# Opening of an attention-plus-SwiGLU kernel: two load queues, one kvz evacuation, num/den ahead, filler matmuls, and weights gated by k

## The chip, the cores and the metric

The kernel runs on one core of one Trainium2 chip. The metric is device microseconds of one execution. "Before" has a median of 342.39 us. A "span" is the time between the first and last instruction of the profiled execution; it is about 2 us shorter than the time of the same run.

## The reference, cut to what matters

```python
def phi(x, c, s):                       # c, s: cos and sin of pi/2 * position / 576
    r = np.maximum(x, 0.0)
    return np.concatenate([r * c, r * s], axis=-1)      # 64 -> 128 features
kv  = np.einsum('bhsf,bhsd->bhfd', phi(k), v)           # 8 batches, 8 heads, 576 positions
z   = np.sum(phi(k), axis=2)
num = np.einsum('bhsf,bhfd->bhsd', phi(q), kv)
den = np.einsum('bhsf,bhf->bhs', phi(q), z)[..., None] + 1e-06
x   = (num / den)                                       # -> 4608 tokens x 512
xn  = x / rms(x) * rms_g
out = (silu(xn @ w_gate) * (xn @ w_val)) @ w_out        # 512 -> 1536 -> 512
```

## The kernel before

The program is a short opening for batch 0 and then a long stretch in which TensorE (PE in the profile) works on the gate, value and output matmuls, with the attention of the later batches between them. In the opening nothing can overlap with an earlier batch. Its steps are: load q, k and v; scale q (`qp`), transpose it on PE (`tps`), copy it out (`qpT`); scale k (`kp`), cast v (`vv`); compute k times v with z as a 65th column (`kvz`), copy it out (`kvzs`); compute numerator and denominator of four 128-row tiles (`nd`), divide (`den`, `rec`, `xt`), take the sum of squares (`scr`, `rs`), normalise (`xn`), transpose (`tpx`), copy (`xnT`); then the first gate and value matmuls, 128 columns at a time.

```python
    for e in range(4):
        load_piece("q", q, 0, 2 * e, 2, nc.sync)          # all loads on SyncE's queue
    for e in range(2):
        load_piece("k", k, 0, HH * e, HH, nc.sync)
    # ... the 64 last rows of k and v, then four pieces of v, then rms_g ...
    nc.gpsimd.tensor_copy(out=gate[:, :], in_=raws["v", 0][:, 2, 0:1])   # weights wait for v
    load_wgv(0)                                            # 512 columns of w_gate and of w_val
    load_wgv(512)
    load_first("q", 1)
    load_first("k", 1)
    # ... tables; PSUM pools: gv 2 x 2 banks, acc 2 x 1, att 1 x 2 ...
    q_scale(0, 0, V, A); q_scale(0, 1, V, A); q_scale(0, 2, V, A)
    q_tr_pe(0, 0); q_out(0, 0, V)
    q_scale(0, 3, V, A)
    for j, eng in ((1, A), (2, V), (3, A)):
        q_tr_pe(0, j); q_out(0, j, eng)
    # ... k_prep and v_prep, shared by VectorE (V) and ScalarE (A) ...
    for e in range(4):                                     # two heads, evacuate, two heads, ...
        kvz(0, 2 * e, 2)
        kvz_out(0, e % 2, V if e % 2 else A, slice(e // 2, e // 2 + 1))
    nd(0, 0); x_of(0, 0)                                   # one PSUM buffer ("att") for nd
    nd(0, 1); x_of(0, 1)
    nd(0, 2); xn_scale(0, 0); x_of(0, 2)
    # ... xn_tr_pe, xn_out, nd(0, 3), x_of(0, 3), first_steps(0 to 3) interleaved ...
```

## Time and profile before

| what | value | where |
|---|---|---|
| time, median | 342.39 us | runs |
| PE busy over the span | 92% | page |
| PE busy from 0 to 25 us | 9.3 us of 25 | windows of 5 us |
| last piece of q lands | 6.63 us | landing times in the trace |
| kvz of batch 0, four rounds with evacuations | 14.87 to 19.22 us | chain of waits |
| first full-width (512-column) gate matmul | 31.46 us | chain of waits |

The windows view gives, for each stretch in us, the busy time and instruction count of each engine, then the granted PE clock (1.00 is full), the DMA share and GB/s. Its column heads and three rows of the kernel before:

```profile
core 0: us, PE busy (x) PEld busy (x) DVE busy (x) ACT busy (x) POOL busy (x), PEclk, DMA share, GB/s
15.00:20.00 5.00, 3.25 (x48) 2.64 (x45) 1.04 (x4) 0.97 (x3) 2.65 (x4) 0.50 1.18 191
20.00:25.00 5.00, 2.08 (x25) 1.49 (x26) 4.02 (x11) 1.63 (x5) 1.12 (x2) 0.50 1.25 209
25.00:30.00 5.00, 4.95 (x61) 4.62 (x59) 2.85 (x6) 3.20 (x8) 3.09 (x5) 0.64 1.05 396
```

PE is busy 3.25 and then 2.08 us of 5, at half clock, and still mostly at half clock when it has enough to do from 25 us on. Pieces of the chain of waits of the kernel before (start us, duration us, what):

```profile
15.56 0.28 ACT kvzs L149
...
15.88 0.72 PE kvz L226 x10
...
19.26 0.61 PE nd L255 x8
...
19.90 0.18 DVE den L265
...
20.10 0.21 DVE rec L270
...
20.34 0.70 DVE xt L273
...
21.09 0.64 PE nd L255 x8
...
26.65 0.42 PE vps L341 x4
...
31.46 0.38 PE gps L341
```

Each kvz round waits for the copy of the round before, and each nd waits for the division of the tile before, since both use the same PSUM buffer. Four 128-column matmuls take 0.42 to 0.43 us, 0.107 us each.

### The profile page before, as it was taken

Reading aid. Unit: us, or ns where it says so; the run is one execution under the profiler, and the core shown is the slowest. Engines: PE = TensorE matmul, PEld = TensorE weight load, DVE = VectorE, ACT = ScalarE, POOL = GpSimd, SP = SyncE. Lnnn points to the kernel's source line nnn. Section 1 sums busy time; section 2 is a strip of 40 time slices with the busy share of each in tenths; the row PEclk is TensorE's granted clock in tenths of the full one; section 3 lists DMA queues with packets and bytes.
Section 4 is the critical chain, followed back from the end, with each engine's and each line's share of the span. In section 5 each row is a group of like instructions: output and inputs, shape, how many; then the busy total and the mean of one; then the engine's idle time right before and its main releaser. Section 6 shows DMA issues by size and latency. Waiting matters only on the chain.

```text
span 340.3 us, 5633 instructions
## 1 busy us (share of the span) xinstructions
PE 313.8 (92%) x2060; PEld 159.3 (47%) x2096; DVE 193.1 (57%) x423; ACT 152.3 (45%) x300; POOL 40.8 (12%) x69
## 2 busy tenths in 40 slices
PE   1459999899899998999999999999999999999994
PEld 1447555455445444544544455445544444444441
DVE  4754577766687896589268945792674132132300
ACT  4626773864444463443444444444443223323221
POOL 0528451101100110110011001100110000000000
PEclk9858999999999999999999999999999999999999
DMA  7999998448849799659948895691113100000024
GB/s 236 242 215 310 297 341 247 120 109 280 297 112 215 185 188 231 201 129 233 243 130 162 187 259 173 138 205 64 45 32 64 62 31 33 31 31 34 31 63 92
DMA packets 81757, 53.59 MB, mean 157 GB/s; under 512 B 52097, under 2 KB 75137, under 8 KB 81729
## 3 DMA queue, kind: packets, MB, share of 16 engines
q1 hardware_dynamic: 74864, 40.91, 46.2%
q0 software_dynamic: 6864, 12.32, 14.4%
q8 instruction: 16, 0.26, 0.3%
q14 instruction: 13, 0.10, 0.1%
HBM read 38.01 MB, written 9.44 MB: 139 GB/s over the span
## 4 chain that ended last, share of the span: by engine, by line
PE 78%; DVE 12%; ACT 3%; issue 3%; DMA 1%; SPq 0%; DVEq 0%; ACTq 0%
PE gps L341 24%; PE vps L341 24%; PE acc L378 20%; PE kvz L226 3%; DVE hT L350 3%; DVE xt L273 3%; PE nd L255 3%; DVE xn L294 2%; DVE kp L142 2%; PE acc L649 2%; PE tps L197 1%; ACT scr L281 1%; ACT sil L349 1%; DMA raw<-in_q_dram 1%; DVE rec L270 1%
## 5 line engine op out<-in xcount | busy, mean ns | idle before, releaser
L350 DVE TENSOR_TENSOR hT<-vps,sil 128x512 bf16<-128x512 f32 x108 | 74.5, 691 | 106.8 <-PE vps L341 77.5
L341 PE MATMUL gps<-xnT,wg 128*128 128x512 bf16 (+1 forms) x437 | 111.3, 370 | 1.2 <-issue 0.2
L341 PE MATMUL vps<-xnT,wv 128*128 128x512 bf16 (+1 forms) x447 | 111.5, 370 | 0.5
L378 PE MATMUL acc<-wo,hT 128*128 128x512 bf16 x378 | 96.6, 379 | 1.7 <-DVE hT L350 1.5
L349 ACT ACTIVATE sil<-gps 128x512 bf16<-128x512 f32 x108 | 63.3, 591 | 66.1 <-PE gps L341 61.8
L341 PEld LDWEIGHTS <-wv 128*128 128x128 bf16 x456 | 44.1, 99 | 50.0
L341 PEld LDWEIGHTS <-wg 128*128 128x128 bf16 x456 | 41.7, 99 | 40.8 <-issue 0.2
L378 PEld LDWEIGHTS <-hT 128*128 128x128 bf16 x384 | 37.5, 98 | 47.2 <-DVE hT L350 2.5
L281 ACT ACTIVATE scr<-xt 128x513 bf16<-128x513 f32 x36 | 22.9, 635 | 65.0 <-DVE xt L273 65.0
L286 POOL TENSOR_TENSOR rs<-ssq,mhalf 128x1 f32<-128x1 f32 x36 | 20.1, 557 | 195.5 <-ACT scr L281 195.5
L149 ACT COPY osb<-acc 128x512 f32<-128x512 f32 x34 | 19.9, 584 | 25.6 <-PE acc L378 23.6
L294 DVE SCALAR_TENSOR_TENSOR xn<-xt,rs,gb 128x512 bf16<-128x512 f32 x36 | 26.7, 743 | 0.8 <-POOL rs L286 0.8
L273 DVE TENSOR_TENSOR xt<-nd,rec 128x512 f32<-128x512 f32 x36 | 24.9, 691 | 1.2
L255 PEld LDWEIGHTS <-qpT 128*128 128x128 bf16 x256 | 12.6, 102 | 11.5 <-DVE xt L273 3.6
L255 PE MATMUL nd<-kvzs,qpT 128*128 128x65 bf16 x256 | 14.2, 200 | 3.6 <-DVE xt L273 3.0
L142 DVE TENSOR_SCALAR qp<-raw,cos_tab 128x512 bf16<-128x512 f32 x32 | 15.0, 480 | 3.5 <-DMA raw<-in_q_dram 3.5
L226 PE MATMUL kvz<-vv,kp 128*128 128x65 bf16 x256 | 12.0, 199 | 4.5 <-DVE vv L151 3.4
L149 ACT CAST vv<-raw 128x512 bf16<-128x512 f32 x26 | 14.8, 619 | 2.6 <-DMA raw<-in_v_dram 2.6
L142 DVE TENSOR_SCALAR kp<-raw,cos_tab 128x512 bf16<-128x512 f32 x32 | 15.2, 482 | 0.0
L226 PEld LDWEIGHTS <-kp 128*128 128x128 bf16 x320 | 11.8, 101 | 6.7 <-ACT kp L140 3.5
L197 PE MATMUL tps<-ident,qp 128*128 128x128 bf16 x64 | 6.3, 265 | 7.7 <-ACT qp L140 7.5
L649 PE MATMUL acc<-wo,hT 128*128 128x512 bf16 x46 | 11.4, 379 | 0.1
(65 smaller groups left out, 154.7 us busy)
## 6 DMA issues: line engine op xcount, KB each, us to landing
out_dram<-osb SPq DMA_DIRECT2D x32, 256.0 KB, 2.5
raw<-in_q_dram SPq DMA_DIRECT2D x20, 256.0 KB, 4.0
raw<-in_v_dram SPq DMA_DIRECT2D x20, 256.0 KB, 3.3
raw<-in_k_dram SPq DMA_DIRECT2D x16, 256.0 KB, 4.5
raw<-in_k_dram SPq DMA_DIRECT2D x4, 512.0 KB, 6.2
raw<-in_q_dram POOLq DMA_DIRECT2D x2, 1024.0 KB, 12.3
raw<-in_k_dram POOLq DMA_DIRECT2D x2, 1024.0 KB, 13.7
raw<-in_v_dram POOLq DMA_DIRECT2D x2, 1024.0 KB, 10.7
```

Source lines behind the costliest of these rows:

```text
L142: nc.vector.tensor_scalar(out=dst, in0=src, scalar1=tab[lanes, col : col + 1], scalar2=0.0, op0=ALU.mult, op1=ALU.max,)
L149: nc.scalar.copy(out=dst, in_=src)
L226: nc.tensor.matmul(kvz_ps[b][:, h // 2 % 2, c0 : c0 + DE], lhsT=kp[:, c, h, :], rhs=vv[:, c, h, :] if c < NJ else vvr[:, b % 2, h, :], sta ...
L255: nc.tensor.matmul(ps[rows, h // HH, (h % HH) * DE : (h % HH + 1) * DE], lhsT=src[:, h, cols], rhs=kz[:, h, :], start=True, stop=True,)
L273: nc.vector.tensor_tensor(out=xt[:, 0:DM].rearrange("p (g h d) -> p g h d", g=2, d=D), in0=ndv[:, :, :, 0:D], in1=rec[:, :].rearrange("p ( ...
L281: nc.scalar.activation(out=scr[:, :], in_=xt[:, :], func=AF.Square, scale=DM**-0.5, accum_out=ssq[:, :],)
L286: nc.gpsimd.tensor_tensor(out=rs[:, :], in0=ssq[:, :], in1=mhalf[:, :], op=ALU.pow)
L294: nc.vector.scalar_tensor_tensor(out=t[:, :], in0=xt[:, 0:DM], scalar=rs[:, 0:1], in1=gb[:, :], op0=ALU.mult, op1=ALU.mult,)
L341: nc.tensor.matmul(ps[:, c0 : c0 + n], lhsT=w[:, dt, nn * P : (nn + 1) * P], rhs=xnTs[blk][:, dt, c0 : c0 + n], start=(dt == 0), stop=(dt ...
L349: nc.scalar.activation(out=sil[:, :], in_=gps[:, :], func=AF.Silu)
L350: nc.vector.tensor_tensor(out=hTs[blk][:, nn, :], in0=vps[:, :], in1=sil[:, :], op=ALU.mult)
L378: nc.tensor.matmul(acc[:, :], lhsT=hTs[blk][:, nn, j * P : (j + 1) * P], rhs=wo[:, nn, :], start=(nn == 0), stop=(nn == NNT - 1),)
```

## The change

Its intent is to shorten the opening. q and k of batch 0 go over two queues (SyncE's and ScalarE's). kvz of all heads runs in one go, with one evacuation; the kept layout of `kvzs` follows PSUM, so that the later batches too evacuate in one instruction instead of two. PSUM pools are opened and closed so that num/den of batch 0 has three buffers and can run ahead of the division. Filler matmuls on a tile of zeros keep PE busy. The weight loads wait for k, which is loaded before v, and come in smaller chunks first.

```diff
-        load_piece("q", q, 0, 2 * e, 2, nc.sync)
+        load_piece("q", q, 0, 2 * e, 2, nc.scalar if e % 2 else nc.sync)
-        load_piece("k", k, 0, HH * e, HH, nc.sync)
+        load_piece("k", k, 0, HH * e, HH, nc.scalar if e % 2 else nc.sync)
-    nc.gpsimd.tensor_copy(out=gate[:, :], in_=raws["v", 0][:, 2, 0:1])
-    load_wgv(0)
+    nc.gpsimd.tensor_copy(out=gate[:, :], in_=raws["k", 0][:, HH, 0:1])
+    load_wgv(0, 256)
+    load_wgv(256, 256)
+    def keep_warm(n, pool="fill"):
+        ps = pools[pool].tile([P, SM], FP32, name="fill", tag=pool)
+        for _ in range(n):
+            nc.tensor.matmul(ps[:, :], lhsT=ident[:, :], rhs=zeros[:, :], start=True, stop=True)
+    with open_psum("fill", 1) as pools["fill"]:
+        keep_warm(12)
         ... q_scale, q_tr_pe, q_out as before, with
+            keep_warm(2)                  # before each of the transposes 1, 2 and 3
+        keep_warm(8)                      # after them
         ... k_prep, v_prep as before ...
-    for e in range(4):
-        kvz(0, 2 * e, 2)
-        kvz_out(0, e % 2, V if e % 2 else A, slice(e // 2, e // 2 + 1))
-    nd(0, 0); x_of(0, 0); nd(0, 1); x_of(0, 1); nd(0, 2); ... nd(0, 3); ...
+    with open_psum("nd", 2) as pools["nd"]:
+        kvz(0, 0, H, "nd")
+        kvz_out(0, V)
+        keep_warm(2, "acc")
+        nd(0, 0, "nd"); nd(0, 1); nd(0, 2, "nd")
+        x_of(0, 0); x_of(0, 1)
+        nd(0, 3)
+        x_of(0, 2)
+        keep_warm(8, "acc")
+    pools["gv"] = ctx.enter_context(open_psum("gv", 2))
     ... xn, transposes and first_steps follow, each first_steps one transpose later ...
-                kvz_out(b, 0, A)          # later batches
-                kvz_out(b, 1, V)
+                kvz_out(b, A)
```

(The diff is cut: the change of the `kvzs` index in `nd` and the order of the last x and xn are left out.)

## The prediction

> What bounds the kernel now. The kernel is a short opening (batch 0 loaded, q transposed, kvz, num/den, normalisation) and then a long TensorE stretch. The stretches of 5 us show PE busy 4.9 to 5.0 of 5 us from 25 us on; from 0 to 25 us it is busy only about 9 of 25. The first full-width step starts at 31.46 us (timeline, chain of waits). After that the kernel is PE-bound (page: PE 92%), so what ends the opening earlier comes off the end nearly one for one, if the loads keep up.
>
> The opening in the chain of waits: q lands at 6.63 us; q scaling, transposes and their copies, then k and v preparation on VectorE and ScalarE until 14.8; kvz in four rounds, each 0.72 us of PE and 0.28 to 0.30 of evacuation, 14.87 to 19.26 (4.4 us); three rounds of num/den, each waiting for the one PSUM buffer (nd 0.62, den 0.18, rec 0.21, xt 0.70: 1.85 us) to 24.78; then PE work at half clock. The windows give a granted clock of 0.50 from 15 to about 28.6 us: 8 transposes take about 0.85 us there and 0.45 later.
>
> What the change does, costed:
> 1. Two load queues. Issues on SyncE are 0.46 us each, and the DMA rate sags to about 200 GB/s from 3.5 to 5.2 us against 380 later. I expect q 0.7 to 1.2 us earlier (5.5 to 5.9). ScalarE's table load (1.28 us) moves behind three issues, still in time.
> 2. Fillers. 12 from about 2.3 us, cold some 5 us, can hold the first transposes by up to 1 us, but bring full clock by 6 to 9 us. [...] the clock rises at 28.6 after a window with PE about 98% busy, and the windows before it, 45 to 65% busy, did not raise it. Transposes and copies: about 1 us less.
> 3. kvz in one go: 1.25 us (as for batch 1 at 50.68) plus one evacuation, estimate 0.75 us from 0.29 (130 columns) and 0.44 (260): 2 us in place of 4.4.
> 4. num/den ahead: VectorE becomes the bound: 4 x 1.13 (x) + 4 x 0.75 (xn) = 7.5 us plus the tail, all PE work hidden at full clock.
> 5. Weights gated by k instead of v: about 3 us earlier[...]. v can land no earlier than the 13.5 of now, perhaps later: I charge 0.5 us.
>
> Sum: kvz starts about 13.5 (14.87), ends evacuated 15.6 (19.2), last xn about 23.5 (28.8), full-width steps start at 26.2 (31.46). Batch 1's single evacuation on ScalarE saves another 0.2. The later loads (first chunk of w_gate to w_out) stay continuous and come some 3 us earlier; their slack now is 3.5 to 9 us, so I expect no new wait. Gain about 5.3 us: 337.1 us, range 335.0 to 339.6.
>
> What would show it: clock 1.0 from some point before 10 us and no 0.50 later; kvz evacuation near 0.75 us; VectorE without gaps from kvz to the last xn; the first full-width gate matmul at 25.5 to 27; the rest of the trace merely shifted.
>
> What would make it wrong: weights starving v (kvz starting after 15); clock lost again in the idle time before kvz; fillers delaying the transposes; q of batch 1 landing later than its use at about 27 us; ScalarE, not VectorE, pacing k.
>
> Chances: faster by over 2% 0.15, within 2% 0.83, slower 0.02.

The 0.5 us charged in term 5 is guess alone, with no number behind it. The "6 to 9 us" of term 2 is an estimate. It can be worked out from the kernel before, whose clock records lie 3.41 us or a multiple of it apart (11.56, 14.97 and 28.63): one or two such steps after the start of the fillers at 2.3 us.

## The result

The changed kernel took 337.74 us (337.35 to 338.36, 4 runs) against 342.39 us, a ratio of 0.9862 with a 95% interval of 0.9841 to 0.9884. Ratios here are the mean time of one kernel's fast runs over that of the other's of the same rounds, so not quite the ratio of the medians that are quoted. The prediction of 337.1 us, in a range of 335.0 to 339.6 and most likely within 2%, held.

The same rows of the windows view of the changed kernel:

```profile
15.00:20.00 5.00, 2.88 (x55) 1.96 (x52) 3.76 (x11) 1.45 (x4) 2.90 (x5) 1.00 1.40 197
20.00:25.00 5.00, 3.88 (x53) 3.08 (x51) 3.64 (x7) 3.00 (x7) 3.24 (x6) 1.00 1.21 252
25.00:30.00 5.00, 4.98 (x51) 3.25 (x49) 2.26 (x4) 3.06 (x6) 3.52 (x5) 1.00 1.06 370
```

The clock is full in these three stretches (its first record in this trace, at 6.22 us, is a rise), and VectorE is busy where it was idle (3.76 us in place of 1.04 from 15 to 20 us). The chain of waits of the changed kernel:

```profile
2.27 4.68 PE fill L463 x12
6.96 0.45 PE tps L198 x8
...
12.99 1.08 ACT vv L150 x2
...
14.13 1.38 PE kvz L230 x40
...
15.53 0.71 DVE kvzs L152
...
16.29 0.42 PE nd L258 x8
...
19.38 1.73 PE fill L463 x8
21.11 0.24 PE tpx L318 x4
...
27.04 1.02 PE gps L344 x4
```

The first full-width matmul starts at 27.04 us, 4.42 us earlier. From there on the trace is the old one, shifted: the twelve products of gate and value of batch 0 (`hT` on VectorE) are each 4.43 us earlier than in the old trace, nearly all of the next block 4.68, the last 4.76. The step from 4.43 to 4.68 is batch 1, whose two evacuations ran one after the other before (0.38 us on ScalarE, then 0.44 on VectorE, in the chain of waits at 51.95 us) and are one now.

So in this pair of executions 4.4 of the 4.8 us come from the opening. The open questions were which parts of the change earn them, and why the opening was 0.8 us longer than predicted (27.04 in place of 26.2). Two theories of the gain were tested. Theory 1: the clock earns most of it, and the restructuring little. Theory 2: the removed waits earn it, and the fillers are decoration.

### The profile page after: what moved, and what is told of

It reads as the page before. It is cut to its first block, busy times and chain, and to the rows that moved or that the text cites. A ratio compares the mean times of both kernels' runs of the same rounds, so it can differ in the third digit from the quotient of the medians.

```text
span 335.6 us, 5731 instructions
## 1 busy us (share of the span) xinstructions
PE 318.9 (95%) x2132; PEld 157.9 (47%) x2132; DVE 190.6 (57%) x416; ACT 153.0 (46%) x298; POOL 43.1 (13%) x71
## 3 DMA queue, kind: packets, MB, share of 16 engines
q10 hardware_dynamic: 1072, 1.05, 0.9%
## 4 chain that ended last, share of the span: by engine, by line
PE 80%; DVE 12%; ACT 4%; issue 2%; DVEq 0%; ACTq 0%
PE gps L344 24%; PE vps L344 24%; PE acc L381 21%; DVE hT L353 3%; PE kvz L230 3%; DVE xt L276 3%; PE fill L463 2%; DVE xn L297 2%; PE nd L258 2%; PE acc L664 2%; ACT sil L352 1%; ACT scr L284 1%; PE tps L198 1%; DVE rec L273 1%; DVE kp L143 1%
## 5 line engine op out<-in xcount | busy, mean ns | idle before, releaser
L258 PEld LDWEIGHTS <-qpT 128*128 128x128 bf16 x256 | 11.5, 97 | 9.8 <-issue 2.4
L258 PE MATMUL nd<-kvzs,qpT 128*128 128x65 bf16 x256 | 12.9, 193 | 2.2 <-DVE xt L276 1.8
L463 PE MATMUL fill<-zeros,ident 128*128 128x512 bf16 x36 | 10.8, 444 | 2.3 <-DVE warm L411 2.3
L230 PE MATMUL kvz<-vv,kp 128*128 128x65 bf16 x256 | 10.8, 193 | 2.3 <-ACT vv L150 2.3
L230 PEld LDWEIGHTS <-kp 128*128 128x128 bf16 x320 | 10.7, 97 | 4.4 <-ACT vv L150 2.8
```

What stands on the lines that cost most here:

```text
L230: nc.tensor.matmul(kvz_ps[b][:, slot_of(h)[0], c0 : c0 + DE], lhsT=kp[:, c, h, :], rhs=vv[:, c, h, :] if c < NJ else vvr[:, b % 2, h, :], ...
L258: nc.tensor.matmul(ps[rows, h // HH, (h % HH) * DE : (h % HH + 1) * DE], lhsT=src[:, h, cols], rhs=kz[:, slot_of(h)[0], slot_of(h)[1], :], ...
```

## The experiments

In every experiment the number read from the profiled execution is the start of the first full-width gate matmul, called F below (31.46 us before, 27.04 in the changed kernel). The part of the span behind F is nearly the same in all traces (308.5 to 309.1 us), so nearly all of the spread between the runs of a kernel, 1 us and more, lies in the opening and is in F: one F stands for its execution, not for its kernel. The profiled execution of the kernel before took 342.11 us, faster than six of the seven that were run beside experiments 1 to 4 (341.84 to 343.51). Where one execution's F and the times of several runs disagree, both are told.

### 1. The changed kernel without fillers

```diff
     def keep_warm(n, pool="fill"):
-        ps = pools[pool].tile(...); for _ in range(n): nc.tensor.matmul(...)
+        return
```

> The changed kernel with every filler matmul taken out, all else kept. Theory 1 (the clock carries most of the gain): the granted clock is 0.5 for most of the opening, kvz takes about 2.3 us in place of 1.38, the 128-column gate and value matmuls run at about 107 ns, and the first full-width step starts at 29.5 to 30.5 us in place of 27.04: 340.2 to 341.3 us. Theory 2 (the removed waits carry it, the fillers are decoration, since VectorE paces num/den and x): at most 1 us later, 338 to 338.8 us.

Measured: 340.59 us (339.90 to 341.82), 0.994 of before (0.9907 to 0.9973); F = 30.88 us. The chain of waits of this run:

```profile
14.62 2.37 PE kvz L230 x40
...
22.32 0.62 PE tpx L318 x4
...
24.19 0.43 PE vps L344 x4
...
30.88 1.02 PE gps L344 x4
```

kvz takes 2.37 us in place of 1.38, and the small gate and value matmuls 0.107 us each. VectorE delivers the first xn at 22.27 us, but PE then needs 8.5 us (22.32 to 30.86) for what takes it 5.9 us in the changed kernel. Without the clock, the waits that the change removes win 0.6 us of the 4.4 in this pair of executions, and about 2.1 us (0.9 to 3.2) by the times of all runs (the ratio 0.994 and its interval, applied to 342.9 us). Theory 2 falls: it expected 338.8 us at most. (Not all of F's loss is the clock: VectorE's seven k instructions took 3.45 us here and 3.17 in the changed kernel.) (The windows view prints a clock of 1.00 for 10 to 25 us of this run, though its first clock record is at 29.2 us: a stretch before the first record is printed as full. The durations of the matmuls show the truth.)

### 2. The kernel before with fillers alone, twice

```diff
+    keep_warm(12)                          # into the still unused "att" buffer
     ...
     for j, eng in ((1, A), (2, V), (3, A)):
+        keep_warm(2)
         q_tr_pe(0, j); q_out(0, j, eng)
+    keep_warm(8)                           # second try: keep_warm(18)
     ...
+    keep_warm(2, "acc")                    # before nd(0, 0) and after nd(0, 0), (0, 1), (0, 2)
```

> The kernel before with fillers alone (12 first, 2 before each later transpose, 8 after, 2 around each num/den), all waits, the single queue and the order kept. Theory 1: the clock stays at 1.0 from 6 or 7 us on, the first full-width step comes 3 to 3.8 us earlier, at 27.7 to 28.5 us: about 338.6 to 339.4 us. Theory 2: PE still waits in each of the four kvz rounds and for the one num/den buffer, so at most 1 us is won: 341.4 us or more.

Measured: 340.86 us (340.47 to 341.60), 0.9947 (0.9922 to 0.9972); F = 30.96. By the trace's clock records (each has the time of a change and the new clock) it rose at 8.0 us, fell at 14.85, just as kvz began, and rose again only at 21.7: the fillers ended at 12.8 us, and PE was then idle until 14.85. The test of theory 1 was spoiled, so it was repeated with 18 fillers there.

> The kernel before with fillers again, now 18 in place of 8 after the q transposes, so that PE isn't idle before kvz (in the first try the clock fell at 14.85 us after an idle window). Theory 1 (clock): 1.0 from before 10 us on without a break, kvz rounds 0.40 us in place of 0.72, the first full-width step at 27.8 to 28.8 us (31.45 before): 338.7 to 339.8 us. Theory 2 (waits): it stays above 30 us even at full clock: 341 us or more.

Measured: 340.43 us (340.16 to 340.83), 0.9928 (0.9911 to 0.9945); F = 29.58, with full clock from 4.9 us on. The chain of waits:

```profile
15.00 0.47 PE kvz L227 x10
...
15.49 0.28 ACT kvzs L150
...
15.81 0.47 PE kvz L227 x10
...
29.58 0.38 PE gps L342
```

The clock alone wins 1.9 us by F, less than theory 1 expected (2.7 to 3.7), and about 2.5 us (1.9 to 3.1) by the times. So neither theory holds by itself: neither half earns what both earn together, 4.4 us by F, and by the times 4.7 us (4.0 to 5.4) in the first call of the changed kernel and 4.1 (3.4 to 4.7) in a second one (experiment 5). Whether the two are worth more together than the sum of each is not shown. The single executions say so (0.6 and 1.9 against 4.4), the times do not (2.1 and 2.5 against 4.1 to 4.7); the execution of the kernel before that F is compared with was a fast one, and the one without fillers (341.17 us) the second slowest of its four. What the traces do show is why neither half suffices: with the old order PE waits for evacuations that the clock didn't shorten (0.28 us on ScalarE at half clock in the kernel before, 0.28 at full clock in this run); with the new order and the old clock PE has its inputs earlier and becomes the bound itself.

### 3. The last eight fillers

In the changed kernel's chain the first xn transpose starts at 21.11 us, when the last eight fillers end, though its xn was ready at 20.59 (the timeline has it from 19.85 for 0.74 us). Do they only cost?

```diff
-        keep_warm(8, "acc")
```

> The changed kernel without the last 8 fillers, which in its trace hold the first xn transpose until 21.11 us though xn was ready at 20.6. If they only cost: clock still 1.0, the transpose starts at 20.65 and the first full-width step 0.3 to 0.5 us earlier (26.6): about 337.3 us. Rival (they keep the clock): the clock falls to 0.5 after 19 us and the first full-width step comes 1 us or more later: 338.7 us or more.

Measured: 341.25 us (339.40 to 342.71), 0.9953 (0.9911 to 0.9995); F = 31.94. But this execution had another trouble first. The VectorE timelines of the changed kernel and of this run, over the preparation of k:

```profile
9.81 1.80 DVE L143 TENSOR_SCALAR kp<-raw,cos_tab 128x512 bf16<-128x512 f32 x4
11.53 0.61 DVE L143 TENSOR_SCALAR kp<-raw,sin_tab 128x512 bf16<-128x512 f32 x1
```

```profile
10.72 3.01 DVE L143 TENSOR_SCALAR kp<-raw,cos_tab 128x512 bf16<-128x512 f32 x4
13.65 0.82 DVE L143 TENSOR_SCALAR kp<-raw,sin_tab 128x512 bf16<-128x512 f32 x1
```

Four instructions took 3.01 us in place of 1.80. In the same stretch GpSimd issued the weight loads, and the GpSimd timeline has an issue of w_val at 0.76 us here, at 0.92 us in the changed kernel:

```profile
10.49 0.76 POOL L127 DMA_DIRECT2D wv<-in_moe_w_val_dram  x1
```

One engine's instructions are longer where the other's are shorter. What causes this was not shown. In the changed kernel the same engines overlap in the same stretch, and VectorE isn't slowed that much (0.47 to 0.61 us an instruction). k was then late, kvz started only at 17.13 us, and the clock had been lost at 14.9, after a window of 3.41 us with PE busy 1.17 us of it (34%). The question about the fillers was put again with the weights gated by v, which takes GpSimd's work out of that stretch.

### 4. Weights gated by v again

```diff
-    nc.gpsimd.tensor_copy(out=gate[:, :], in_=raws["k", 0][:, HH, 0:1])
-    load_wgv(0, 256)
-    load_wgv(256, 256)
+    nc.gpsimd.tensor_copy(out=gate[:, :], in_=raws["v", 0][:, 2, 0:1])
+    load_wgv(0)
```

> The changed kernel with the weights gated by the second v piece and loaded in chunks of 512 columns again, as before. Theory: the first weights land by about 20.5 us, before their first use at 22.0, and the later loads have slack, so the first full-width step stays at 27.0 and the time within 0.3 us of the changed kernel: 337.5 to 338.1 us. Rival (the opening ends earlier only because the weights do): the first gate matmuls wait for a load, 1 to 3 us later, 338.7 to 340.7 us.

Measured: 337.25 us (336.74 to 338.59), 0.9843 (0.9805 to 0.988); F = 27.37. The first weights landed at 17.9 and 21.4 us, before their first use at 22.34, and no gate matmul waited for a load. So gating by k buys nothing in this opening. In this execution the seven k instructions took 2.98 us, as in the kernel before.

> Weights gated by v again (as the changed kernel was run before, at 337.25 us), and the last 8 fillers out. If those fillers only cost: clock stays 1.0 from before 10 us on, the first xn transpose starts about 0.4 us earlier relative to the last num/den, and the first full-width step at 26.9 to 27.1 us (27.37 with them): about 336.9 us. Rival (they keep the clock): it falls back to 0.5 near 20 to 23 us and the time is 338.5 us or more.

Measured: 338.86 us (338.75 to 340.02), 0.9888 (0.9867 to 0.9909); F = 28.23. The first xn transpose did start earlier, at 21.02 (21.45 with the fillers), but the clock was halved from 21.18. Windows of this run, cut at its clock records and in steps of 3.41 us from them (experiment 5 tells where this length is from):

```profile
14.36:17.77 3.41, 2.71 (x66) 2.21 (x66) 1.61 (x5) 0.25 (x1) 3.15 (x4) 1.00 1.06 165
17.77:21.18 3.41, 0.58 (x11) 0.47 (x12) 3.24 (x10) 2.17 (x6) 1.12 (x2) 1.00 1.24 207
21.18:24.60 3.42, 2.75 (x28) 2.58 (x27) 2.86 (x5) 1.34 (x4) 2.25 (x4) 0.50 1.24 207
```

After a window with PE busy 0.58 of 3.41 us the clock is halved for one window. All five runs had a mean clock of 0.993 or less, the four with the fillers 0.994 or more. The last fillers keep the clock; the expectation that they only cost was wrong.

### 5. The changed kernel a second time

> The changed kernel once more, as a control on the same chip as the runs beside it. In the run without the last fillers VectorE's k preparation took 0.82 us an instruction in place of 0.48 to 0.61, while GpSimd issued the weight loads, and the clock was lost. Theory: this comes from gating the weights by k (both engines at work from 9.6 to 15 us) and strikes some executions of the changed kernel too: its times spread over more than 1.5 us, some 2 to 4 us above the fastest. Rival (it came with leaving the last fillers out, or by chance): all within 1 us of 337.7.

Measured: 339.05 us (338.12 to 339.21), 0.9881 (0.9862 to 0.9901), F = 28.79. Neither expectation fits well. The spread is 1.1 us, and VectorE's k instructions were normal (0.48 to 0.61 us), but all four times lie above three of the first four. By the ratios to the kernel before, the two calls aren't clearly apart (0.9841 to 0.9884 and 0.9862 to 0.9901). The times go with the clock. In the mean over the span, one window of 3.41 us at half clock costs 0.005 (half of 3.41 us in 337). Time before the first clock record counts as full, so a low mean shows a loss, and a high one doesn't exclude a late first rise:

| first call, us | mean granted clock | second call, us | mean granted clock |
|---|---|---|---|
| 337.35 | 0.998 | 339.21 | 0.988 |
| 337.65 | 0.998 | 339.20 | 0.992 |
| 337.83 | 0.998 | 338.89 | 0.988 |
| 338.36 | 0.994 | 338.12 | 0.998 |

The windows of this profiled execution, cut in the same way, and then two of the first one, cut in steps of 3.41 us from its rise at 6.22 us:

```profile
12.06:15.47 3.41, 1.24 (x41) 1.27 (x42) 2.35 (x6) 2.00 (x4) 3.41 (x5) 1.00 1.22 188
15.47:18.89 3.42, 2.40 (x31) 1.54 (x27) 2.43 (x7) 0.70 (x2) 1.78 (x2) 0.50 1.41 194
18.89:22.30 3.41, 2.83 (x14) 1.41 (x16) 3.27 (x9) 1.48 (x5) 1.67 (x3) 0.50 1.26 203
```

```profile
9.63:13.05 3.42, 2.19 (x16) 0.99 (x14) 3.42 (x9) 2.92 (x5) 3.21 (x5) 1.00 1.01 330
13.05:16.46 3.41, 1.97 (x48) 1.60 (x49) 1.96 (x5) 1.01 (x2) 3.41 (x5) 1.00 1.28 175
```

Both executions do the same work and have nearly the same gap without PE work before kvz, 2.3 us in the first and 2.5 in the second (timeline of PE). In the first the boundary at 13.05 cuts that gap in two, and no window falls under 48% (1.65 of 3.41 us, from 16.46 to 19.87). In the second nearly all of the gap lies within one window, which is 36% busy (1.24 of 3.41), and the clock is halved for 6.8 us. Then the fillers themselves cost: the chain of waits of the second execution has

```profile
20.09 2.77 PE fill L463 x7
22.86 0.24 PE tpx L318 x4
```

so the first xn transpose starts 1.75 us later than in the first execution, which is all of the difference in F (28.79 against 27.04). About 1.0 us of it is the fillers (2.77 us for seven records, one of the eight missing, in place of 1.73), the rest the half-clock work before them. The length of the windows is read from the clock records: the stretches between two of them are multiples of 3.41 us (3.41 and 13.65 us in the kernel before, from 11.56 to 14.97 to 28.63; 6.83 here, from 15.47 to 22.30; 3.42 in the run without the last fillers of experiment 4, from 21.18 to 24.60). The first rise lies between 4.9 and 8.1 us in the kernels with fillers (6.22 in the changed kernel, 8.0 and 4.9 in the two of experiment 2), so the steps fall differently on the same work from execution to execution.

### 6. One load queue again

```diff
-    load_piece(..., nc.scalar if e % 2 else nc.sync)
+    load_piece(..., nc.sync)               # q and k, on the kernel of experiment 4
```

> Weights gated by v, and all loads on one queue again. Theory: q lands at 6.6 us in place of 5.7, k and v at 9.8 and 13.5 as with two queues; the first 12 fillers end at 7.5 us in most runs, so the first transpose, which could start at 7.4, is not later, and the loss is 0.5 us at most: 337.3 to 337.8 us. Rival (earlier q is what carries the opening): 0.8 us or more later, 338.1 us or more.

Measured: 338.19 us (337.85 to 339.38), 0.9868 (0.9846 to 0.989); F = 28.09, against 27.37 with two queues. The 0.72 us are not the queue's: kvz starts at 14.52 here and at 14.47 there, and what follows is longer because the clock was lost from 15.19 to 18.60 in this execution (kvz 1.84 us in place of 1.38). q lands at 6.6 in place of 5.7 us, but with two queues the first transpose had to wait for the twelve fillers until 7.55, and here it starts at 7.45. By its number the rival's expectation (338.1 us or more) was met, but not by its cause. In these two executions two queues win next to nothing, since the fillers end that late. Two runs at a clock of 0.998 and 0.999 took 337.85 and 337.90 us; a cost of some tenths is not excluded.

### 7. A version with no thin window

Taken over all traces so far, windows with PE busy for 43% or more had kept the clock, and windows with 41% or less had lost it. The changed kernel goes down to 32% in a window that starts between 10.5 and 12 us, and to 38% in one that starts near 15.8. On the kernel of experiment 4:

```diff
-        keep_warm(8)                       # after the q transposes
+        keep_warm(13)
         ...
         nd(0, 0, "nd"); nd(0, 1); nd(0, 2, "nd")
         x_of(0, 0); x_of(0, 1)
+        keep_warm(4, "acc")
         nd(0, 3)
         x_of(0, 2)
-        keep_warm(8, "acc")
+        keep_warm(5, "acc")
```

> A version meant to beat both: weights gated by v, 13 fillers in place of 8 after the q transposes, 4 between the third and the fourth num/den, 5 in place of 8 after it. Over all runs the clock was kept after windows of 3.41 us with PE busy 43% or more and lost at 41% or less; the changed kernel falls to 32% in a window that starts between 10.5 and 12 us and to 38% near 15.8[...]. Theory: here no window falls under 45%, the clock is 1.0 from before 10 us on in every execution, the first full-width step at 26.5 to 27.0 us, and five times within 1 us of each other, 0.9815 to 0.984 of before. Rival (the spread has another cause): again a spread of over 1 us and executions with a mean clock under 0.992.

Measured: 336.74 us (336.58 to 337.81, 4 runs), 0.983 (0.9808 to 0.9851), with mean clocks of 0.997 to 1.000; F = 26.54. Its windows, in steps of 3.41 us:

```profile
10.15:13.56 3.41, 2.89 (x15) 1.15 (x13) 3.41 (x9) 3.23 (x5) 1.82 (x3) 1.00 0.75 271
13.56:16.97 3.41, 2.64 (x66) 2.27 (x68) 1.82 (x6) 0.66 (x2) 3.41 (x5) 1.00 0.89 124
16.97:20.39 3.42, 2.38 (x18) 0.85 (x15) 3.28 (x9) 2.02 (x6) 1.50 (x3) 1.00 1.24 205
```

None is under 70%, and the first xn transpose starts at 20.44, 0.05 us after its xn, in place of 0.5 us. One of the four runs lay 1.2 us above the fastest at a mean clock of 1.000, a little more than the expected 1 us; its cause is open. The interval lies below that of the changed kernel's second call (0.9862 to 0.9901) and overlaps that of its first. It overlaps that of experiment 4 too (0.9805 to 0.988), so what the added fillers win over gating by v alone is not shown by the times; experiment 4's windows fell to 44% and 53%.

The first half of this remedy alone, on the changed kernel:

```diff
-        keep_warm(8)
+        keep_warm(12)
```

> The changed kernel with 12 in place of 8 fillers after the q transposes and nothing else. Theory (idle window before kvz): the clock no longer falls near 15 us; kvz takes 1.38 us; the first full-width step at 26.9 to 27.3 us; median 0.983 to 0.987 of before, better than the 0.9881 of the changed kernel in its second call. Rival (more fillers hold kvz, or the window is not the cause): no better than 0.988, kvz starting after 14.3 us.

Measured: 338.56 us (337.86 to 341.89, 6 runs), 0.9889 (0.9856 to 0.9922); F = 28.59. A miss. The clock did stay past kvz, which took 1.36 us, but it fell at 19.52, after a window of 44% that held the wait for the fourth nd:

```profile
16.11:19.52 3.41, 1.51 (x34) 1.24 (x34) 2.70 (x10) 1.29 (x4) 1.24 (x2) 1.00 1.41 201
```

Then the last eight fillers took 3.12 us. Three of the six runs kept a mean clock of 0.997 or more and took 337.86 to 338.12; the run of 341.89 had 0.989. So both thin stretches must be filled. The 44% of this window also contradicts the edge as just stated: the run of experiment 4 with the fillers kept its clock at 44% (1.50 of 3.41 us, from 10.87 to 14.28), and the one without the last fillers at 43% (1.46 of 3.42, from 10.94 to 14.36). In these traces the edge is somewhere between 41 and 44% as PE's modelled busy time reads, not sharp in it.

### 8. The removed waits, one at a time, on that version

```diff
-        kvz(0, 0, H, "nd")
-        kvz_out(0, V)
+        for e in range(4):                 # two heads, then their evacuation, A and V in turn
+            kvz(0, 2 * e, 2, "nd")
+            copy(V if e % 2 else A, ...)   # 128x130
```

> The version above with kvz in four rounds and four evacuations again. At full clock a round is 0.40 to 0.47 of PE and 0.28 to 0.30 of evacuation plus 0.1 of handover: 3.1 us in place of 1.38 + 0.71 + 0.1 = 2.2. Theory: the first full-width step 0.7 to 1.0 us later than in the version above. Rival (PE has slack there): under 0.3 us.

Measured: 338.69 us (338.46 to 339.13), 0.9881 (0.9858 to 0.9903), F = 28.12: 1.6 us later than in the version above, more than expected. From the start of kvz to the start of the first nd it took 3.45 us (14.37 to 17.82) in place of 2.16 (13.91 to 16.07), so 1.3 us are the rounds themselves; some 0.5 more had come before kvz, where this execution's first fillers ended later, and its first nd was 0.16 shorter.

```diff
-        nd(0, 0, "nd"); nd(0, 1); nd(0, 2, "nd")
+        nd(0, 0); nd(0, 1); nd(0, 2)       # one PSUM buffer
```

> The version above with num and den of batch 0 in the one old PSUM buffer, so that each waits for the x of the tile before it. Theory: VectorE waits 0.45 to 0.6 us before each of three x, and the first full-width step comes 1.0 to 1.6 us later than in the version above. Rival (VectorE has slack): under 0.4 us.

Measured: 339.94 us (339.80 to 340.41), 0.9919 (0.990 to 0.9938), F = 30.09: 3.6 us later, more than twice the expectation (about 3.1 us by the times). The chain shows the wait, 0.44 us of nd between two divisions:

```profile
17.31 0.70 DVE xt L276
...
18.06 0.44 PE nd L258 x8
...
21.35 0.62 PE nd L258 x8
21.98 2.13 PE fill L462 x5
24.11 0.30 PE tpx L318 x4
```

That adds up to 1.2 us from the first nd to the end of the third x (16.43 to 21.31, 4.88 us, in place of 16.07 to 19.7). From there to the first xn transpose it takes 2.80 us (21.31 to 24.11) in place of 0.74 (19.70 to 20.44). Two things are in this. The fourth nd and the five fillers behind it now come after the third x, where the version above had done them beside it. And the clock: PE, waiting for VectorE, was busy 41% of the window from 17.28 to 20.69 with no gap over 1.22 us, the clock fell, and the fillers took 2.13 us where two at full clock take 0.43. The clock is about 1.25 us of the 2.06 in this execution (0.2 in the nd, 1.05 in the fillers). Over the four runs it doesn't decide: two with a mean clock of 0.997, too high for a lost window, took 339.93 and 339.94 us, two with 0.993 and 0.994 took 339.80 and 340.41. Why those two were no faster has no trace and stays open.

## Why the prediction was right, point by point

- Total and chances: right. 4.65 us were won, 5.3 predicted. That the median came within 0.7 us of the prediction is partly luck: three of the first four executions kept the clock, and the second call's median was 339.05 us.
- "Batch 1's single evacuation ... saves another 0.2": right, 0.25 us.
- "no new wait" in the later loads: right, the shift of the later trace is constant to 0.1 us but for batch 1's step and four single products.
- kvz "2 us in place of 4.4": right, 1.38 plus 0.71, 2.16 with the handovers.
- "VectorE becomes the bound ... 7.5 us": right in size, 16.73 to 24.15, with one gap of 0.44 us. But it isn't alone in setting the end: the last eight fillers held the first xn transpose for 0.5 us.
- "kvz starts about 13.5": 14.13. This is the mis-sized term. q did land earlier (5.80 us, within 5.5 to 5.9), but k landed at 9.78, where it was 9.83, and v at 13.41, where it was 13.53. Two queues brought q forward and not k and v. Before kvz two strands end together: VectorE, which starts k's preparation right at k's landing (9.81), has its first vv at 13.98; ScalarE, which comes from the copies of q's transposes (the last from 10.13 to 11.14), ends its vv at 14.06. Which of the two would have to be cut first was not tested. 0.63 of the 0.84 us that F missed lie here.
- "v can land no earlier than ... now, perhaps later: I charge 0.5 us": the charge was for the wrong thing. The first packets of the weight queue moved only after 12 us (34 packets from 12 to 13 us, none from 11 to 12), and v landed no later (13.41, where it was 13.53). What one trace shows instead is VectorE slower while GpSimd issued the loads, in the preparation of k (four instructions in 3.01 us in place of 1.80).
- "clock 1.0 from some point before 10 us and no 0.50 later": right in the profiled execution, wrong as a property of the kernel. In four of eight executions the mean clock was 0.994 or less. The prediction named it as a risk ("clock lost again in the idle time before kvz") and gave it no weight in the time. What it missed is that a window needs not be idle for the clock to fall; in these traces every full-clock window that was 41% busy or less lost it, and one at 44%.

## What to carry to other kernels

Where PE waits between bursts, compute the PE-busy share of every window at every phase (3.41 us in these traces), not the length of the longest gap. Here windows at 41% or less lost the clock and windows at 43 and 44% kept or lost it; the same kernel kept it in one execution, where the steps left no window under 48%, and lost it in another, where one came to 36%. A time measured in a few runs may be that luck. Fillers belong where PE waits, in number as small as the share needs, since at half clock a filler ahead of real work took twice the time (0.85 us for two, 0.43 at full clock). Neither removing the waits nor raising the clock earned the gain alone: about 2.1 and 2.5 us by the times, 4.1 to 4.7 us together. And one profiled execution is no measure of a kernel whose spread lies in the very stretch that is compared.

## What these traces show of the clock and of VectorE

- Loss of the clock: 2.2 us without PE work in a window of 3.41 us were enough (36% busy, second execution of the changed kernel), and in the run with one PSUM buffer two gaps of which none was over 1.22 us (41%), as were windows at 17% (experiment 4 without the last fillers), 34% (experiment 3), 39% (experiment 2, first try), another at 41% (experiment 6) and once 44% (12 fillers, experiment 7). Windows at 43% and 44% (both of experiment 4), 48% (the changed kernel) and more kept it.
- Rise of the clock: windows of 66 and 70% (2.26 and 2.40 of 3.41 us, in the kernel before and in the second execution of the changed kernel) did not raise it; 80 and 83% did (2.75 of 3.42 us in experiment 4 without the last fillers, 2.83 of 3.41 in the second execution of the changed kernel), but in the run without fillers one of about 80% did not (22.38 to 25.79 us; its first clock record is at 29.2).
- Transposes and the clock: in the kernel before, the only PE work before 11.56 us is 32 transposes (`nc.tensor.transpose`, against the identity), and the clock rose at 11.56, after a window in which they kept PE busy 3.20 of 3.41 us.
- VectorE while weight loads are issued: in one execution (experiment 3) instructions that prepare bf16 from float32 with a scalar, 128x512, took 0.82 to 0.98 us in place of 0.48 to 0.61, and the issues of GpSimd 0.76 us in place of 0.92.
- The clock printed for a stretch before the first clock record is not a measurement: it read 1.00 in a run whose matmuls took 0.107 us each until 29.2 us.
